# Top-32 attention and a highway layer on one core: the engines' order written out by hand, the penalty's factor moved into a matmul, two FFN products moved to VectorE

## The chip, the cores and the metric

The kernel runs on one core of a Trainium2 chip. That core has five engines with a queue each: TensorE (PE, with a row of its own for the loads of the stationary operand, PEld), VectorE (DVE), ScalarE (ACT), GpSimd (POOL) and SyncE (SP, which issues the DMA transfers here). An engine works through its queue in order. If the instruction at the head waits for another engine, everything behind it waits too. The metric is the device time of one execution in microseconds (us).

## The reference

There are 8 batches of 8 heads with 576 rows and head size 64, all float32. In each row of scores the 32 largest are kept, a softmax runs over them, and the result multiplies v. The heads, side by side, give 4608 rows of 512 numbers, the input x of the highway layer.

```python
scores = scale * np.matmul(q, k.transpose(0, 1, 3, 2))
kth = np.partition(scores, -top_k, axis=-1)[..., -top_k:-top_k + 1]
scores = np.where(scores >= kth, scores, -1000000000.0)
attn = np.exp(scores - max);  attn = attn / (sum + 1e-09)
x = (attn @ v), heads side by side
H = np.maximum(x @ w_h, 0.0)
T = 1.0 / (1.0 + np.exp(-(x @ w_t + b_t)))
out = T * H + (1.0 - T) * x
```

## The kernel before

The 576 rows of a batch are cut into four groups of 128 rows and a rest of 64. In a full group a tile is one head, in the rest group it is two heads stacked on the 128 partitions. Two tiles make a pair. A full group has 4 pairs and the rest group 2, so a batch has 18 pairs and the program 144, in 40 groups. The number `n` of a pair is its step.

These are the stages of pair `n`, with the step of the program text at which each is written:

- `scores` (step n): PE multiplies q and k into two PSUM tiles `ps` (L132), and ACT takes their positive part into `z` (L145).
- `tree` (n): DVE takes the elementwise larger of the two halves of a row, `hi`, and again of its halves, `hh` (L156, L157). POOL makes the smaller ones, `hl` and `lo`, with integer arithmetic (L161 to L164).
- `lists` (n + 1): DVE finds the 32nd largest with a chain of MAX8 and MATCH_REPLACE8 over `hh`, `hl` and `lo`, for the two tiles by turns (L176 to L197). It then multiplies it by 2^100 into `sthr` (L239).
- `settle` (n + 2, after the last pair of a group): three small POOL instructions note whether the short cut held. If it had not, an exact version would run at the end of the program. It does not run here.
- `mask` (n + 2): ACT makes a penalty `pen`, relu(2^100 * threshold - 2^100 * z), which is zero where the score is kept (L282).
- `trans` (n + 3): PE transposes `z` into PSUM (L295) and takes `pen` off with a second matmul against `nident`, minus the identity (L300), 20 matmuls in all. ACT takes exp into `et` (L312, L322).
- `av` (n + 4): PE multiplies by v, which carries a column of ones for the row sum, and ACT copies the result to `xs` (L352).
- `norm` (n + 5) and `ffn` (n + 6), after the last pair of a group: DVE takes the reciprocal of the sum and halves it (L361, L362), POOL scales to `x` (L364), PE transposes `x`, multiplies by the two weight matrices, and ACT takes relu into `h2` and tanh into `tt` (L398, L408). POOL then combines them with four instructions (L410 to L414) and SP stores the rows.
- `prep` (four times per batch): SP loads two heads of q, k and v, PE transposes q and k, ACT copies them to `kT` and `qT` and casts v.

The transposes of `prep` and all products of `ffn` share one PSUM tile, the only buffer of the pool `fps`.

The text above is not the order of the queues. A scheduler of the recording layer takes the instructions with their dependences and sorts them by a priority of its own, so on each engine stages of neighbouring steps stand mixed.

Of the kernel before, what the change touches and what calls it, by code (L numbers as in the profile page):

```python
# [23 lines left out]

class Group:
# [15 lines left out]
class Ops:  # L41


    def __init__(self, ctx, tc, shared, exact):
        self.tc, self.nc = tc, tc.nc
# [73 lines left out]
    def scores(self, n, g, pi, prep):  # L119
# [7 lines left out]
        for s0, s1 in ((0, 512), (512, S)):  # L127
            for ti, heads in enumerate(g.pairs[pi]):
                for hi, h in enumerate(heads):
# [6 lines left out]
                    )  # L136
        if self.exact:
# [8 lines left out]
        self.st[n] = dict(sc=sc)  # L146

    def tree(self, n):
# [16 lines left out]
        self.st[n]["tree"] = (hh, hl, lo)  # L165
# [52 lines left out]
    def lists(self, n, g, pi):  # L218
        nc, P, S, H = self.nc, self.P, self.S, self.H
        if pi == 0:  # L220
            for name in ("m1", "m4") if self.exact else ("m1", "m2", "m4"):
                setattr(g, name, self.lpool.tile([P, H, 8], FP32, tag=name, name=name))
            if not self.exact:
                g.sthr = self.lpool.tile([P, H], FP32, tag="sthr", name="sthr")
                g.w2 = self.lpool.tile([P, H, S // 4 + 24], FP32, tag="w2", name="w2")
# [4 lines left out]
        else:  # L230
            hh, hl, lo = self.st[n].pop("tree")
# [6 lines left out]
        if not self.exact:  # L238
# [22 lines left out]
    def mask(self, n, g, pi):  # L261
        nc, P, S = self.nc, self.P, self.S
        sc = self.st[n].pop("sc")
        z = self.zbufs[n % NZ]
        pen = None if self.exact else self.pens[n % NPEN]
        for ti in range(2):
# [14 lines left out]
            else:  # L281
# [4 lines left out]
                    bias=g.sthr[:, t : t + 1],  # L286
                    scale=-STEEP,
# [68 lines left out]
    def norm(self, g):  # L356
# [5 lines left out]
        nc.vector.tensor_scalar_mul(rinv[0:ql, :], rinv[0:ql, :], 0.5)  # L362
# [8 lines left out]
    def ffn(self, g, dst):  # L371
        nc, P = self.nc, self.P
        n_g, dm = self.n_g, self.dm
        wh, wt = self.wh, self.wt
        ql = g.qlen
        x = g.x
        xtps = self.fps.tile([P, 512], FP32, tag="fp", name="xtps")
        for i in range(n_g):
            nc.tensor.transpose(  # L379
                xtps[:, i * P : i * P + ql],  # L380
                x[0:ql, i * P : (i + 1) * P],
                self.ident[0:ql, 0:ql],
            )
        xT = self.fpool.tile([P, n_g, P], BF16, tag="xT", name="xT")
        nc.scalar.copy(
            xT[:, :, 0:ql], xtps[:].rearrange("p (g j) -> p g j", j=P)[:, :, 0:ql]
        )
        hps = self.fps.tile([P, 512], FP32, tag="fp", name="hps")
        for i in range(n_g):
            nc.tensor.matmul(  # L390
                hps[0:ql, :],
                xT[:, i, 0:ql],
                wh[:, i, :],
# [3 lines left out]
        h2 = self.fpool.tile([P, dm], FP32, tag="h2", name="h2")  # L397
        nc.scalar.activation(h2[0:ql, :], hps[0:ql, :], AF.Relu)  # L398
        tps = self.fps.tile([P, 512], FP32, tag="fp", name="tps")
        for i in range(n_g):  # L400
            nc.tensor.matmul(
                tps[0:ql, :], xT[:, i, 0:ql], wt[:, i, :], start=(i == 0), stop=False
# [4 lines left out]
        tt = self.fpool.tile([P, dm], FP32, tag="tt", name="tt")  # L407
        nc.scalar.activation(tt[0:ql, :], tps[0:ql, :], AF.Tanh)  # L408
        s1 = self.fpool.tile([P, dm], FP32, tag="s1", name="s1")
# [3 lines left out]
        o = self.fpool.tile([P, dm], FP32, tag="o", name="o")  # L413
        nc.gpsimd.tensor_add(o[0:ql, :], s1[0:ql, :], h2[0:ql, :])  # L414
        nc.sync.dma_start(dst, o[0:ql, :])
# [3 lines left out]
def kernel(  # L419
# [31 lines left out]
    nc.vector.tensor_scalar_mul(nident[:], ident[:], -1.0)  # L451
# [34 lines left out]
    with ExitStack() as cm:  # L486
        ops = Ops(cm, tc, shared, exact=False)

        def load_weights():
            for src, dst in ((moe_w_h, wh), (moe_w_t, wt)):  # L490
                for i in range(0, n_g, 2):
                    w32 = ops.fpool.tile([P, 2, dm], FP32, tag="w32", name="w32")
# [4 lines left out]
                    nc.gpsimd.tensor_copy(dst[:, i : i + 2, :], w32[:])  # L497
            bt32 = ops.fpool.tile([P, dm], FP32, tag="bt32", name="bt32")
# [3 lines left out]
            nc.sync.dma_start(bt32[:], bt_bcast)  # L502
# [41 lines left out]
        for n, (g, pi) in enumerate(pairs):  # L544
# [4 lines left out]
            if end:  # L549
                at(n + 2, ops.settle, g)  # L550
# [89 lines left out]
```

## Time and profile before

| | |
|---|---|
| three runs | median 1320.95 us (1317.99 to 1330.01) |
| the profiled execution | 1329.07 us, of which the span of the trace is 1327.3 |
| mean granted TensorE clock | 0.80 of full speed |
| busy: PE, DVE, ACT, POOL | 1031.8, 942.9, 730.7, 951.7 us |

Busy time is the time in which at least one instruction of an engine runs. Where an engine has been idle, the profile names the instruction of another engine that released it. The granted clock has two levels, 0.5 (1.2 GHz) and 1.0 (2.4 GHz), so 0.80 is a mean over stretches of both. 144 steps in 1327.3 us are 9.2 us per step.

### The profile page before, as it was taken

The page shows a single profiled execution, that of the slowest core. Times are in us where ns is not written, and L with a number is a line of the kernel's source. Part 1 is how long each engine was busy: PE and PEld are TensorE (multiplying, and loading weights), DVE is VectorE, ACT ScalarE, POOL GpSimd, SP SyncE. Part 2 cuts the span into 40 slices and gives each one's busy share as a digit, 9 for nine tenths or more (in the row PEclk, how much of TensorE's full clock was granted, in tenths as well). Part 3 has the DMA queues.
Part 4 walks back from the last instruction along what each step waited for, and adds up shares of the span by engine and source line. Part 5 has one row for each costly group of instructions (what it writes and reads, how often), then busy time and mean ns, then how long its engine had stood idle before and what let it go on. Part 6 is the DMA issues. An engine that isn't in the chain of part 4 may idle for free.

```text
span 1327.3 us, 21095 instructions
## 1 busy us (share of the span) xinstructions
PE 1031.8 (78%) x6569; PEld 599.3 (45%) x6601; DVE 942.9 (71%) x4266; ACT 730.7 (55%) x1465; POOL 951.7 (72%) x922
## 2 busy tenths in 40 slices
PE   5779796787798876878878888787876778866764
PEld 3445453444445443454444544454443444434432
DVE  6768757787677777777668776588775796676663
ACT  4566555555656555565554655565564565544442
POOL 5777867678777776777775777767677777776774
PEclk9787867878868877789786777787877888877786
DMA  4422111111101111111010111011110100000000
GB/s 103 132 56 49 26 36 31 27 26 27 44 23 27 35 26 36 22 45 27 22 31 23 41 30 31 22 23 44 27 27 13 31 15 9 9 13 9 8 9 15
DMA packets 123336, 41.56 MB, mean 31 GB/s; under 512 B 117456, under 2 KB 117456, under 8 KB 123216
## 3 DMA queue, kind: packets, MB, share of 16 engines
q1 hardware_dynamic: 123216, 40.14, 12.1%
q8 instruction: 54, 0.88, 0.3%
q14 instruction: 66, 0.54, 0.1%
HBM read 30.67 MB, written 9.44 MB: 30 GB/s over the span
## 4 chain that ended last, share of the span: by engine, by line
POOL 38%; PE 30%; DVE 19%; issue 6%; ACT 5%; SPq 1%; DMA 0%; POOLq 0%; ACTq 0%
POOL lo L163 10%; PE ps L132 10%; POOL lo L164 5%; PE zt L295 5%; POOL hl L161 5%; POOL s L410 4%; POOL hl L162 4%; DVE w L189 4%; PE hps L390 3%; DVE w L195 3%; POOL h L411 3%; PE zt L300 3%; DVE m L197 2%; DVE m L192 2%; PE xtps L379 2%
## 5 line engine op out<-in xcount | busy, mean ns | idle before, releaser
L132 PE MATMUL ps<-kT,qT 64*128 64x64 f32 (+3 forms) x1280 | 427.2, 518 | 12.3 <-ACT z L145 11.0
L282 ACT ACTIVATE pen<-z,sthr 128x576 bf16<-128x576 f32 x288 | 209.3, 770 | 276.4 <-DVE sthr L239 274.6
L295 PE MATMUL zt<-ident,z 128*128 128x128 f32 x1152 | 322.4, 336 | 0.0
L163 POOL TENSOR_TENSOR lo<-z,hi 128x576 int32<-128x576 int32 x144 | 222.0, 1546 | 115.1 <-DVE sthr L239 100.5
L300 PEld LDWEIGHTS <-pen 128*128 128x128 bf16 x1440 | 172.8, 123 | 267.5 <-ACT pen L282 235.4
L300 PE MATMUL zt<-nident,pen 128*128 128x128 bf16 x1152 | 256.6, 259 | 42.8 <-ACT pen L282 42.5
L185 DVE MAX8 w<-hl 128x8 f32<-128x72 f32 x288 | 52.4, 222 | 332.7 <-POOL hl L162 332.7
L164 POOL TENSOR_TENSOR lo<-lo,z 128x576 int32<-128x576 int32 x144 | 208.8, 1450 | 3.9
L295 PEld LDWEIGHTS zt<-ident,z 128*128 128x128 f32 x1152 | 193.4, 172 | 30.5 <-issue 5.9
L145 ACT ACTIVATE z<-ps 128x576 f32<-128x576 f32 x288 | 178.3, 650 | 51.3 <-PE ps L132 50.0
L300 PE MATMUL zr<-nident,pen 128*128 128x128 bf16 x288 | 72.1, 258 | 171.8 <-ACT pen L282 170.2
L132 PEld LDWEIGHTS ps<-kT,qT 64*128 64x128 f32 (+1 forms) x1280 | 154.1, 200 | 113.9 <-issue 63.4
L322 ACT ACTIVATE et<-zt 128x512 bf16<-128x512 f32 x288 | 170.1, 597 | 29.6 <-PE zt L300 28.1
L410 POOL TENSOR_TENSOR s<-h,x 128x512 f32<-128x512 f32 (+1 forms) x40 | 64.8, 1620 | 159.6 <-ACT h L398 159.4
L156 DVE TENSOR_TENSOR hi<-z 128x576 f32<-128x576 f32 x144 | 115.3, 803 | 19.7 <-ACT z L145 19.3
L189 DVE MAX8 w<-lo 128x8 f32<-128x288 f32 x288 | 115.4, 441 | 7.6 <-POOL lo L164 7.6
L161 POOL TENSOR_TENSOR hl<-hi,hh 128x288 int32<-128x288 int32 x144 | 116.9, 821 | 1.0 <-DVE sthr L239 1.0
L162 POOL TENSOR_TENSOR hl<-hl,hi 128x288 int32<-128x288 int32 x144 | 113.1, 794 | 0.0
L344 PEld LDWEIGHTS <-et 128*128 128x128 bf16 (+1 forms) x1600 | 79.0, 109 | 56.5 <-ACT z L145 15.4
L157 DVE TENSOR_TENSOR hh<-hi 128x288 f32<-128x288 f32 x144 | 103.1, 753 | 0.1
L312 ACT ACTIVATE et<-zr 128x256 bf16<-128x256 f32 x144 | 55.4, 385 | 79.5 <-PE zr L300 71.2
L344 PE MATMUL zr<-v,et 128*128 128x65 bf16 (+1 forms) x1600 | 97.9, 205 | 1.6 <-ACT et L322 1.1
(78 smaller groups left out, 1645.6 us busy)
## 6 DMA issues: line engine op xcount, KB each, us to landing
kin<-in_k_dram SPq DMA_DIRECT2D x64, 128.0 KB, 2.6
qin<-in_q_dram SPq DMA_DIRECT2D x64, 128.0 KB, 2.6
vin<-in_v_dram SPq DMA_DIRECT2D x64, 128.0 KB, 2.6
out_dram<-o SPq DMA_DIRECT2D x32, 256.0 KB, 2.2
kin<-in_k_dram SPq DMA_DIRECT2D x64, 16.0 KB, 2.3
qin<-in_q_dram SPq DMA_DIRECT2D x64, 16.0 KB, 2.3
vin<-in_v_dram SPq DMA_DIRECT2D x64, 16.0 KB, 2.3
w<-in_moe_w_h_dram SPq DMA_DIRECT2D x2, 512.0 KB, 4.5
```

The source lines that it names most:

```text
L132: nc.tensor.matmul(pss[ti][rows, s0:s1], qT[r, h // 2, qs : qs + g.qlen], kT[r, h // 2, s0:s1],)
L145: nc.scalar.activation(sc[:, ti, :], pss[ti][:, 0:S], AF.Relu)
L161: gp.tensor_tensor(hli, hii[:, :, 0:H2], hhi, ALU.subtract)
L162: gp.tensor_tensor(hli, hli, hii[:, :, H2:H1], ALU.add)
L163: gp.tensor_tensor(loi, sci[:, :, 0:H1], hii, ALU.subtract)
L164: gp.tensor_tensor(loi, loi, sci[:, :, H1:S], ALU.add)
L189: vec.max(w2[:, H2 + 16 : W], lo)
L282: nc.scalar.activation(pen[:, ti, 0:S], sc[:, ti, :], AF.Relu, bias=g.sthr[:, t : t + 1], scale=-STEEP,)
L295: self.nc.tensor.matmul(dst, z[:, ti, cs], self.ident[:], is_transpose=True, start=True, stop=pen is None,)
L300: self.nc.tensor.matmul(dst, pen[:, ti, cs], self.nident[:], start=False, stop=True)
L322: nc.scalar.activation(et[:, ti, 0:J, :], zt[:].rearrange("p (c j) -> p c j", c=J), AF.Exp, scale=self.scale,)
L344: nc.tensor.matmul(zr[0:ql, col : col + DE], et[:, ti, c, q0 : q0 + ql], vb[:, h, c, :], start=(c == 0), stop=(c == J),)
```

## The change

First, the order. Every PE, DVE, ACT and POOL instruction of the main path is passed to `tc.keep_in_program_order`, so the queues now stand as the text does. SP's queue is still sorted by the scheduler. The text is rewritten as one loop over steps. In step n stand: the tree and the POOL minima of pair n, the first penalty of pair n-2, `av` of n-3, the second penalty, a `prep` where one is due, scores and `z` of pair n+1, the lists of n-1, one of three FFN jobs, `trans` of n-2, `settle`, `norm`. Line 35 is the wrapper that issues all of these.

Second, the penalty. `pen` is now relu(threshold - z), and the factor 2^100 stands in `nident`. The instruction `sthr` falls away.

Third, the FFN. It is cut into jobs `ffn_x`, `ffn_h` and `ffn_t` with `ffn_o`, one job per step. DVE makes d = max(hps, 0) - x straight from PSUM, ACT writes the tanh back into PSUM, DVE makes d * (tanh + 1), and POOL makes o = (x + x) + d with two instructions. ACT's relu falls away. The halving of the reciprocal falls away too, since v's extra column now holds 2.

The weights are loaded two steps earlier, into four buffers, and cast on POOL one piece per step.

```diff
+class Pinned:
+        def issue(*args, **kw):
+            return self._tc.keep_in_program_order(fn(*args, **kw))
...
-        self.tc, self.nc = tc, tc.nc
+        self.nc = tc.nc if exact else PinnedCore(tc)
...
-            nc.vector.tensor_scalar_mul(
-                g.sthr[:, t0 : t0 + 2], g.m4[:, t0 : t0 + 2, 7], STEEP
-            )
...
-                    bias=g.sthr[:, t : t + 1],
-                    scale=-STEEP,
+                    bias=g.m4[:, t, 7:8],
+                    scale=-1.0,
...
-        nc.vector.tensor_scalar_mul(rinv[0:ql, :], rinv[0:ql, :], 0.5)
...
-        nc.scalar.activation(h2[0:ql, :], hps[0:ql, :], AF.Relu)
+        nc.vector.scalar_tensor_tensor(
+            out=g.d[0:ql, :], in0=hps[0:ql, :], scalar=0.0, in1=g.x[0:ql, :],
+            op0=ALU.max, op1=ALU.subtract,
+        )
...
-        nc.scalar.activation(tt[0:ql, :], tps[0:ql, :], AF.Tanh)
-        nc.gpsimd.tensor_add(s1[0:ql, :], h2[0:ql, :], x[0:ql, :])
-        nc.gpsimd.tensor_sub(h2[0:ql, :], h2[0:ql, :], x[0:ql, :])
-        nc.gpsimd.tensor_mul(h2[0:ql, :], h2[0:ql, :], tt[0:ql, :])
-        nc.gpsimd.tensor_add(o[0:ql, :], s1[0:ql, :], h2[0:ql, :])
+        nc.scalar.activation(tps[0:ql, :], tps[0:ql, :], AF.Tanh)
+        nc.vector.scalar_tensor_tensor(
+            out=g.d[0:ql, :], in0=tps[0:ql, :], scalar=1.0, in1=g.d[0:ql, :],
+            op0=ALU.add, op1=ALU.mult,
+        )
+        gp.tensor_tensor(o[0:ql, :], g.x[0:ql, :], g.x[0:ql, :], ALU.add)
+        gp.tensor_tensor(o[0:ql, :], o[0:ql, :], g.d[0:ql, :], ALU.add)
...
-    nc.vector.tensor_scalar_mul(nident[:], ident[:], -1.0)
+    nc.vector.tensor_scalar_mul(nident[:], ident[:], -STEEP)
...
-        nc.gpsimd.memset(vt[:], 1.0)
+        nc.gpsimd.memset(vt[:], 2.0)
...
+            if have(n):
+                ops.tree(n)
+                ops.minima(n)
+            if have(n - 2):
+                ops.mask(n - 2, *pairs[n - 2], tis=(0,))
+            if have(n - 3):
+                ops.av(n - 3, g, pi, preps[g.b][2])
+            if have(n - 2):
+                ops.mask(n - 2, *pairs[n - 2], tis=(1,))
+            if n in preparing:
+                prep(*preparing[n])
...
+            if have(n + 1):
+                ops.scores(n + 1, g, pi, preps[g.b])
+                ops.evac(n + 1)
+            if have(n - 1):
+                ops.lists(n - 1, *pairs[n - 1])
+            for job in ffn[:1]:
+                job.pop(0)()
...
+            if have(n - 2):
+                ops.trans(n - 2)
...
+                    ops.settle(g)
...
+                    ops.norm(g)
```

POOL's queue before, about one group's FFN (`s1`, `h2`, `o` are its tiles, `z4` and `z5` belong to the next two pairs):

```order
L410 TENSOR_TENSOR s1_1846<-h2_1836,x_1732 128x512
L250 TENSOR_TENSOR room_89<-m4_1477,w2_1479 128x24
L256 TENSOR_TENSOR slack_91<-m2_1476,m4_1477 128x8
L411 TENSOR_TENSOR h2_1836<-h2_1836,x_1732 128x512
L163 TENSOR_TENSOR lo_1815<-z4_73,hi_1814 128x576
L164 TENSOR_TENSOR lo_1815<-lo_1815,z4_73 128x576
L161 TENSOR_TENSOR hl_1817<-hi_1814,hh_1816 128x288
L163 TENSOR_TENSOR lo_1941<-z5_75,hi_1940 128x576
L162 TENSOR_TENSOR hl_1817<-hl_1817,hi_1814 128x288
L412 TENSOR_TENSOR h2_1836<-h2_1836,tt_1844 128x512
L161 TENSOR_TENSOR hl_1943<-hi_1940,hh_1942 128x288
L414 TENSOR_TENSOR o_1850<-s1_1846,h2_1836 128x512
```

The same engine now, two steps and the start of a third, with a group's output (`o`) and the next group's `x`:

```order
L35 TENSOR_TENSOR hl_1449<-hi_1446,hh_1448 128x288
L35 TENSOR_TENSOR hl_1449<-hl_1449,hi_1446 128x288
L35 TENSOR_TENSOR lo_1447<-z1_67,hi_1446 128x576
L35 TENSOR_TENSOR lo_1447<-lo_1447,z1_67 128x576
L35 TENSOR_TENSOR o_1515<-x_1224 128x512
L35 TENSOR_TENSOR o_1515<-o_1515,d_1414 128x512
L35 TENSOR_TENSOR hl_1549<-hi_1546,hh_1548 128x288
L35 TENSOR_TENSOR hl_1549<-hl_1549,hi_1546 128x288
L35 TENSOR_TENSOR lo_1547<-z2_69,hi_1546 128x576
L35 TENSOR_TENSOR lo_1547<-lo_1547,z2_69 128x576
L35 TENSOR_TENSOR x_1632<-xs_1237,rinv_1630 128x512
L35 TENSOR_TENSOR hl_1637<-hi_1634,hh_1636 128x288
```

Before, the minima of two pairs stand between and behind the four FFN instructions, the first of which waits for ACT's relu. Now the four minima of a pair stand together, and what depends on DVE's last work of a step (`o` with `d`, `x` with `rinv`) stands between two steps.

DVE's queue now, at the end of a step with the third FFN job (`m4` ends the chain, `hi` and `hh` begin the next step):

```order
L35 MAX m4_1479<-w3_1501 128x8
L35 MAX m4_1479<-w3_1503 128x8
L35 SCALAR_TENSOR_TENSOR d_1414<-tps_1507,d_1414 128x512
L35 TENSOR_TENSOR hi_1546<-z2_69 128x576
L35 TENSOR_TENSOR hh_1548<-hi_1546 128x288
```

Both FFN products now stand at that place, behind the chain and ahead of the tree, and wait there for PE or ACT.

PE's queue before (`ps_2967` and `ps_2968` are one pair, `ps_3086` is the first tile of the next):

```order
L295 MATMUL zt_2920<-ident_58,z0_65 128x128
L132 MATMUL ps_2967<-kT_740,qT_741 128x512
L295 MATMUL zr_2904<-ident_58,z0_65 128x128
L132 MATMUL ps_2968<-kT_740,qT_741 128x512
L132 MATMUL ps_2967<-kT_740,qT_741 128x64
L132 MATMUL ps_2968<-kT_740,qT_741 128x64
L132 MATMUL ps_3086<-kT_740,qT_741 128x512
L379 MATMUL xtps_2863<-ident_58,x_2775 128x128 x4
```

PE's queue now, in a step with a `prep` and the third FFN job:

```order
L35 MATMUL zr_2843<-v1_85,et_2842 128x65
L35 MATMUL kqps_2910<-ident_58,kin_2895 128x128 x4
L35 MATMUL kqps_2916<-ident_58,qin_2900 128x128 x4
L35 MATMUL kqps_2922<-ident_58,kin_2895 128x64
L35 MATMUL kqps_2922<-ident_58,qin_2900 128x64
L35 MATMUL ps_2929<-kT_715,qT_716 128x512
L35 MATMUL ps_2930<-kT_715,qT_716 128x512
L35 MATMUL ps_2929<-kT_715,qT_716 128x64
L35 MATMUL ps_2930<-kT_715,qT_716 128x64
L35 LDWEIGHTS xT_2749
L35 MATMUL tps_2967<-wt_96,xT_2749 128x512
```

Before, the second tile of the pair that `ps_3086` begins stood some 70 rows further on. Now the two tiles' matmuls are always neighbours, and the transposes of a `prep` stand in one block ahead of them.

## Rows read from the trace of the kernel before

**Rows 1.** The page, busy time, share of the span and instructions of each engine

```profile
PE 1031.8 (78%) x6569; PEld 599.3 (45%) x6601; DVE 942.9 (71%) x4266; ACT 730.7 (55%) x1465; POOL 951.7 (72%) x922
```

**Rows 2.** Waits: who waited for whom, us in total, times, longest us

```profile
DVE w L185 <- POOL hl L162: 332.7, 76, 10.5
ACT pen L282 <- DVE sthr L239: 274.6, 65, 8.9
...
POOL s L410 <- ACT h L398: 159.4, 37, 9.9
```

**Rows 3.** Timeline near the end: start, duration, instruction, [idle before <- releaser]

```profile
1281.73 1.82 POOL L410 TENSOR_TENSOR s<-h,x 128x512 f32<-128x512 f32 x1 [4.65 <-ACT h L398]
...
1291.98 0.37 DVE L185 MAX8 w<-hl 128x8 f32<-128x72 f32 x2 [7.61 <-POOL hl L162]
...
1297.05 0.29 PE L300 MATMUL zr<-nident,pen 128*128 128x128 bf16 x1 [9.34 <-ACT pen L282]
```

**Rows 4.** Timeline of DVE, one chain, then two trees

```profile
553.89 0.51 DVE L176 MAX8 m<-hh 128x8 f32<-128x144 f32 x2
...
556.16 0.37 DVE L185 MAX8 w<-hl 128x8 f32<-128x72 f32 x2 [0.24 <-POOL hl L162]
...
558.98 0.18 DVE L361 RECIPROCAL rinv<-xs 128x8 f32<-128x8 f32 x1
...
564.74 0.75 DVE L156 TENSOR_TENSOR hi<-z 128x576 f32<-128x576 f32 x1
565.40 0.82 DVE L157 TENSOR_TENSOR hh<-hi 128x288 f32<-128x288 f32 x2
566.14 0.51 DVE L176 MAX8 m<-hh 128x8 f32<-128x144 f32 x2
```

**Rows 5.** Timeline of DVE and POOL, trees beside POOL's two-input instructions

```profile
599.27 1.99 POOL L163 TENSOR_TENSOR lo<-z,hi 128x576 int32<-128x576 int32 x1
...
599.92 3.11 DVE L157 TENSOR_TENSOR hh<-hi 128x288 f32<-128x288 f32 x2
...
601.22 1.49 POOL L410 TENSOR_TENSOR s<-h,x 128x512 f32<-128x512 f32 x1
```

**Rows 6.** Groups by line: count, busy us, mean ns, idle us before them

```profile
L189 DVE MAX8 w<-lo 128x8 f32<-128x288 f32 x288 | 115.4, 441 | 7.6 <-POOL lo L164 7.6
...
L414 POOL TENSOR_TENSOR o<-s,h 128x512 f32<-128x512 f32 (+1 forms) x40 | 50.8, 1270 | 0.2
...
L364 POOL TENSOR_TENSOR x<-xs,rinv 128x512 f32<-128x512 f32 (+1 forms) x40 | 41.7, 1042 | 42.5 <-DVE rinv L362 38.1 <-PE ps L132 4.3
...
L239 DVE TENSOR_SCALAR sthr<-m 128x2 f32<-128x2 f32 x144 | 36.9, 256 | 0.1
```

**Rows 7.** Stretches: length, busy us (instructions) of PE, PEld, DVE, ACT, POOL, clock, DMA

```profile
50.00:1300.00 1250.00, 986.24 (x6305) 570.96 (x6337) 905.24 (x4134) 697.59 (x1397) 908.03 (x868) 0.80 0.11 28
602.70:604.27 1.57, 1.57 (x20) 1.32 (x18) 1.57 (x9) 1.33 (x3) 1.57 (x3) 1.00 0.00 0
1297.00:1299.73 2.73, 2.68 (x18) 2.00 (x18) 2.73 (x16) 1.54 (x3) 0.00 (x0) 0.50 0.00 0
```

**Rows 8.** Timeline of PE: gate matmuls, score matmuls of one tile, of two

```profile
601.61 1.04 PE L401 MATMUL tps<-wt,xT 128*128 128x512 bf16 x4
...
605.67 1.12 PE L132 MATMUL ps<-kT,qT 64*128 64x512 f32 x2
...
606.98 1.12 PE L132 MATMUL ps<-kT,qT 64*128 64x512 f32 x4
```

**Rows 9.** Timeline at the start, second `prep` of the program and what follows

```profile
14.22 1.11 PE L98 MATMUL kqps<-ident,kin 128*128 128x128 f32 x4
...
18.11 2.34 PE L132 MATMUL ps<-kT,qT 64*128 64x512 f32 x7
...
20.48 1.19 ACT L145 ACTIVATE z<-ps 128x576 f32<-128x576 f32 x2 [1.55 <-PE ps L132]
```

**Rows 10.** Timeline at the end, last MAX8 of the last chain

```profile
1300.17 0.56 DVE L197 MAX8 m<-w 128x8 f32<-128x168 f32 x2
```

More of the change, by code (lines that the diff above doesn't have):

```diff
@@ L22, with __init__, __getattr__ @@
 NPEN = 3
+class Pinned:
+    def __init__(self, tc, engine):
+        self._tc, self._engine = tc, engine
+    def __getattr__(self, name):
+        fn = getattr(self._engine, name)
+        def issue(*args, **kw):
+            return self._tc.keep_in_program_order(fn(*args, **kw))
+        return issue
+class PinnedCore:
+    def __init__(self, tc):
+        for name in ("tensor", "vector", "scalar", "gpsimd"):
+            setattr(self, name, Pinned(tc, getattr(tc.nc, name)))
+        self.sync = tc.nc.sync
 class Group:
@@ L487 @@
         ops = Ops(cm, tc, shared, exact=False)
+        weights = []
         def load_weights():
@@ L551, with have @@
-        for hp in range(1, NHP):
-            at(hp - 1, prep, 0, hp)
-        at(3, load_weights)
+        preparing = {hp - 1: (0, hp) for hp in range(1, NHP)}
         for b in range(1, B):
             for hp in range(NHP):
-                at(first[b] - 12 + 3 * hp, prep, b, hp)
-        step = 0
-        while todo:
-            for fn, args in todo.pop(step, []):
-                fn(*args)
+                preparing[first[b] - 12 + 3 * hp] = (b, hp)
+        NPR = len(pairs)
+        def have(n):
+            return 0 <= n < NPR
@@ new lines @@
+        prep(0, 0)
+        ops.scores(0, *pairs[0], preps[0])
+        ops.evac(0)
+        ffn = []
+        step = 0
+        while step < NPR + 4 or ffn:
+            n = step
+            if have(n):
[4 more added lines that the diff above has]
+            if have(n - 3):
+                g, pi = pairs[n - 3]
+                ops.av(n - 3, g, pi, preps[g.b][2])
[3 more added lines that the diff above has]
+                prep(*preparing[n])
+            if n == 1:
+                load_weights()
+            if weights and n > 2:
+                cast_weights()
+            if have(n + 1):
+                g, pi = pairs[n + 1]
+                ops.scores(n + 1, g, pi, preps[g.b])
[4 more added lines that the diff above has]
+                job.pop(0)()
+                if not job:
+                    ffn.pop(0)
+            if have(n - 2):
+                ops.trans(n - 2)
+            if have(n - 1):
+                g, pi = pairs[n - 1]
+                if pi == len(g.pairs) - 1:
+                    ops.settle(g)
+            if have(n - 3):
+                g, pi = pairs[n - 3]
+                if pi == len(g.pairs) - 1:
+                    ops.norm(g)
+                    ffn.append(
+                        [
+                            lambda g=g: ops.ffn_x(g),
+                            lambda g=g: ops.ffn_h(g),
+                            lambda g=g: (ops.ffn_t(g), ops.ffn_o(g, out_rows(g))),
+                        ]
+                    )
```

113 lines of the change are left out of this document (61 added, 52 removed).

## The prediction

> **What bounds the kernel now.** I read the busy times first [rows 1]. Over a span of 1327.3 us no engine is above 78%, and three of them stand between 71 and 78%. So no engine is full: they take turns in waiting. The list of waits says for what [rows 2]. DVE stands 332.7 us before the first MAX8 on `hl`, which POOL makes late. POOL itself stands 159.4 us at the head of its queue with the FFN's first instruction, which wants ACT's relu, while the minima that DVE needs are queued behind it. ACT then waits 274.6 us for the threshold.
>
> The timeline shows one such round from end to end [rows 3]. POOL has been idle for 4.65 us when the FFN instruction is released at 1281.73. Minima of two pairs and the rest of the FFN follow, and at 1291.98 DVE resumes after 7.61 us. At 1297.05 PE resumes after 9.34 us. The program's limit is the order in the queues, and each engine pays for it in turn.
>
> **What a step costs when nothing waits.** DVE has the most work per step after the change, so I price a step there. A chain runs from 553.89 to 558.98, with 0.24 us of idle inside: 4.85 us. A `hi` costs 565.40 - 564.74 = 0.66, a `hh` half of 566.14 - 565.40, so 0.37 [rows 4]. A step is 5.88 us, where the program now takes 9.2.
>
> **The change part by part.**
>
> *Start.* The second pair's `z` ended at 20.48 + 1.19 = 21.7 us [rows 9]. Two more steps follow that each wait for a `prep`, which takes 7.45 us from its first transpose to the end of `z` (14.22 to 21.67), and the weights' loads now stand in SP's queue ahead of the last of them. I put the beginning of step 3 at 40 us, between 21.7 + 2 x 7.45 = 36.6 and 45.
>
> *Trees and chains.* 141 trees and 142 chains remain: 141 x 1.03 + 142 x 4.85 = 834 us. `sthr` (36.9 us of DVE [rows 6]) is not in it. It was also the last link before ACT's penalty, about 0.26 us on that path in each step.
>
> *FFN on DVE.* No row shows a DVE product that reads PSUM. The nearest is `hi`, 0.66 us for 576 elements. A MAX8 of 288 takes 0.44 [rows 4, 6], and twice that is 0.88 for 576. The bounds for 512 are 0.5 and 0.8, and I take `hi`'s 0.66. With a reciprocal of 0.18, 40 x (2 x 0.66 + 0.18) = 60 us, between 47 and 71.
>
> ACT loses a relu and POOL two of four FFN instructions of 1.27 us, 40 x 2 x 1.27 = 102 us. Both have room beside DVE's step, so this buys nothing directly. It keeps POOL's load (951.7 - 102 = 850 us, 5.9 per step) just below DVE's.
>
> *Collisions of DVE and POOL.* While POOL ran a `lo` and then `s`, DVE's two `hh` took 3.11 us in place of 0.74 [rows 5, 4]. The first ended only after the `lo` had, the second after `s`. The `lo` in turn started at 599.27, when a `hi` was running, and took 1.99. So a DVE instruction with two SBUF inputs and a POOL one exclude each other, for the whole instruction, by turns. MAX8 with one input does not suffer, 441 ns in the mean although POOL is busy 72% of the time [rows 6, 1].
>
> The new order puts POOL's late work exactly where DVE's tree is. DVE's reciprocal, its second product and the last MAX8 release POOL's `x` (1.04 us), `o` (1.27) and `room` while `hi` runs, and `hh` then waits for the POOL instruction. Ahead of `o` with `d`, the instruction x + x ends about 0.5 us after DVE wants its `hi`. Per group this is 1.04 + 1.27 + 0.5 + 0.2 (my estimate for `room`) = 3.0 us, for 40 groups 120 us. The lower bound is 0, if DVE waits for `z` at that time anyway.
>
> Whether the new products collide too, no row shows. As bounds I take nothing, and 0.7 us for the one that meets x + x, 28 us in all. I take nothing, because one of their inputs is in PSUM, which makes them more like MAX8 than like `hh`. The Trainium skill (SBUF — State Buffer, section Who interferes with whom) says the same of DVE instructions with at most one SBUF input. By it the term is 0, and the sum stays as it is.
>
> *Prepared steps.* 28 steps carry a `prep` of the next batch, and all of its transposes and copies pass through the single `fps` buffer before PE reaches the step's scores. At the low clock that is 7.45 us to the end of `z` [rows 9], and ACT's two penalties stand ahead of the first copy (about 0.7 more): 8.1. At the high clock the score matmuls take 1.12 and not 2.34 [rows 8, 9] and one set of transposes half of 1.11, so 6.4. DVE wants `z` after 5.88, so 0.5 to 2.2 us are lost. In two of a batch's four such steps the gate matmuls (1.3 us from 601.61 to the end of the fifth at high clock, twice that at low) and the tanh stand between, and DVE's product, which waits for them, stands ahead of the tree: 0.7 to 1.9 more. I take 1.8 us in the mean: 50 us, between 25 and 90.
>
> *PE and its clock.* PE's 1031.8 us are 7.2 per step at a mean clock of 0.80 [rows 1, 7]. One part gets cheaper. The score matmuls of one tile alone take 1.12 us, those of two tiles side by side take 1.12 as well [rows 8]. Before they were mostly apart. I take 1.2 us off per step (one 1.12, a little more at low clock), which leaves 6.0 at 0.80. Between `trans` and `av` PE also waits about 1.0 us for the last exp. PE's own round is then 7.0 us at clock 0.80, 5.8 at 1.0 and 10.6 at 0.5. With DVE's 7.1 (5.88 plus FFN and collisions, 180 us over 144 steps) this is no longer cover but a near tie. Slack of some 2.7 us (`z` is ready that long before the tree needs it) hides single slow stretches. I add 15 us, between 0 and 145 (the third case below).
>
> *End.* From the last chain's MAX8 at 1300.17 to the end of the span are 27 us [rows 10]. The same stages follow it now, in the same dependence: 27.
>
> Sum: 40 + 834 + 60 + 120 + 50 + 15 + 27 = 1146 us of span, 1.8 more outside it: 1148 against the profiled 1329.07. The median of the runs shown is 0.6% below that execution, so I forecast **1140 us**.
>
> **The rivals.**
>
> *No collisions.* POOL's late instructions fall beside DVE's chain, or beside waits. For it: a group has one `x`, one `o` and one `room`, so some steps have none of them, and where DVE waits for `z` they cost nothing. Against it: they are released by the very instruction that stands ahead of the tree. 1146 - 120 gives a median near 1020, and less if the prepared steps cost little: 960 to 1060.
>
> *PE's clock stays as mixed as it is.* If 40% of the time goes at 0.5 and the slack doesn't cover it, steps alternate between 7.3 and 10.6 us: 1 / (0.6/7.3 + 0.4/10.6) = 8.3, or 1.0 us more on 141 steps, 1285. For it: PE's rows show 0.80 with 7.2 us of work in a 9.2 us step. Against it: PE now has pauses of about 1 us, not 9.34.
>
> *PE at 1.2 GHz nearly throughout, slower than before.* 20 matmuls of `trans` take 1.57 us in a stretch with the clock at 1.00, and 18 take 2.68 at 0.50 [rows 7]. If the pauses in every step let the clock fall and keep it down, each step takes PE's 10.6 us, and 40 + 141 x 10.6 + 27 gives about 1560. It decides where the mean step passes 9.2 us: a low share of about 0.6, a mean clock under 0.70. The Trainium skill (TensorE: Matmul & The Clock Gate, section Part 4: PE-mode transpose) says that transposes do not bring the full clock, and half of `trans` is transposes. By that rule this case would be the likely one; the stretch at 1.00 was made of `trans` alone, so the trace doesn't bear it out, though it is short.
>
> *The waits only move.* `hi` waits for `z` as long as the MAX8 waited for `hl`, because the fixed order ties all engines to the slowest of each step: 1308 to 1334. Against it: no engine has more than 7.2 us per step.
>
> That the order is not what the text says is excluded by the queues shown.
>
> **How the numbers follow.** Forecast case (1060 to 1200): 0.52. No collisions (960 to 1060): 0.23. Mixed clock (1200 to 1307): 0.17. Low clock: 0.05. Waits move: 0.03. The range of 1010 to 1280 leaves out some 0.08 below, which is part of the second case, and 0.12 above, which is the end of the third and the last two. A difference of 1% is about what can be told from none. Faster: 0.52 + 0.23 + 0.17 = 0.92, same 0.03, slower 0.05.
>
> **What would show it.** DVE's wait for `hl` should be nearly gone and DVE busy above 80% of the span. `hh` should have a mean well above 0.45 us, with the long ones in the steps with `x`, `o` and `room`. If `hh` stays near 0.45, the collisions were wrong. In prepared steps DVE should wait for `z` or for the tanh. The score matmuls should take clearly less than before, and the mean clock should be at least 0.80. The forecast is wrong upward if DVE waits for `z` in most steps and PE is the engine without idle time, and wrong downward if the mean step is below 6.6 us.

## The result, and the profile after

The changed kernel takes **1099.91 us** (median of 4 runs, 1097.74 to 1100.31), the kernel before 1324.61 us on the same chip (4 runs, 1317.99 to 1330.01). The ratio is 0.8302, 95% interval 0.8257 to 0.8348. The forecast was 1140 us, with a range of 1010 to 1280. The profiled execution has a span of 1098.5 us and a mean granted clock of 0.859.

The page, busy time, share of the span and instructions of each engine, as in [rows 1]:

```profile
PE 822.1 (75%) x6562; PEld 549.7 (50%) x6601; DVE 976.7 (89%) x4162; ACT 712.1 (65%) x1425; POOL 839.6 (76%) x842
```

One engine now stands out. DVE has hardly more work than before (976.7 against 942.9 us) but does it in 1098.5 us. It is idle for 121.8 us, where it was idle for 384.4. The page's fourth part, the chain of work that ended last by engine, says the same:

```profile
DVE 70%; PE 17%; ACT 8%; issue 3%; SPq 1%; DMA 1%; POOL 0%; ACTq 0%; DVEq 0%; POOLq 0%
```

The waits (who for whom, us in total, times, longest us), to be set beside [rows 2]:

```profile
POOL hl L35 <- DVE hh L35: 152.7, 117, 9.5
ACT pen L35 <- DVE m L35: 142.7, 81, 3.7
...
DVE hi L35 <- ACT z L35: 45.7, 12, 11.3
...
DVE d L35 <- ACT tps L35: 42.5, 17, 3.5
...
DVE d L35 <- PE hps L35: 19.0, 8, 5.0
```

DVE's 332.7 us for `hl` are gone, and so are POOL's 159.4 us for the relu. The direction has turned: POOL and ACT now wait for DVE, and that costs nothing. What DVE still waits for are `z`, the tanh (`tps`) and the relu's matmuls (`hps`), 107 us together. Of these, 28 us lie in the first four steps and 12 behind the last tree. The others lie in the steps with a `prep` alone. In the batches from the second on, DVE waits 2.94, 3.27, 1.93 and 2.53 us in a batch's four such steps (means); the first batch's four have 3.5 us together. Every other step has 0.04. Over the 28 steps with a `prep` that is 67 us.

One of these steps in the timeline (start, duration, instruction, idle before it):

```profile
478.63 1.12 PE L35 MATMUL kqps<-ident,kin 128*128 128x128 f32 x4 [2.62 <-DVE d L35]
...
480.43 1.11 PE L35 MATMUL kqps<-ident,qin 128*128 128x128 f32 x4 [0.68 <-ACT kT L35]
...
482.48 2.34 PE L35 MATMUL ps<-kT,qT 64*128 64x512 f32 x7
...
484.75 0.61 PE L35 MATMUL tps<-wt,xT 128*128 128x512 bf16 x1
...
487.16 0.58 ACT L35 ACTIVATE tps<-tps 128x512 f32<-128x512 f32 x1 [1.05 <-issue]
...
487.77 0.69 DVE L35 SCALAR_TENSOR_TENSOR d<-tps,d 128x512 f32<-128x512 f32 x1 [3.27 <-ACT tps L35]
...
488.38 0.75 DVE L35 TENSOR_TENSOR hi<-z 128x576 f32<-128x576 f32 x1
```

DVE's list ended at 484.5. On PE the `prep` stands ahead of the scores, and these ahead of the gate matmuls; the tanh follows, and the product waits for it with the tree behind it. So the wait bears the name of the tanh and was made by the `prep`.

PE itself had stood idle for 2.62 us before this `prep`, until DVE's first FFN product had been made and the `fps` buffer was free. From 477.4 to 487.6 the granted clock was 0.50. Over steps 6 to 125 its mean is 0.62 in the steps with a `prep` and 0.94 in the others.

The groups by line (busy us, mean ns, idle before), where `hi` and `hh` are the two instructions of a tree:

```profile
L35 PE MATMUL ps<-kT,qT 64*128 64x64 f32 (+3 forms) x1280 | 244.6, 509 | 0.0
...
L35 DVE TENSOR_TENSOR hi<-z 128x576 f32<-128x576 f32 x144 | 121.7, 845 | 45.7 <-ACT z L35 45.7
...
L35 DVE TENSOR_TENSOR hh<-hi 128x288 f32<-128x288 f32 x144 | 122.9, 854 | 5.0
...
L35 DVE MAX8 w<-lo 128x8 f32<-128x288 f32 x288 | 115.1, 440 | 0.0
```

In steps where POOL does nothing at that time a `hi` takes 0.745 and a `hh` 0.458 us. The rows are 121.7 + 122.9 - 144 x 1.203 = 71 us above that. MAX8 stays at 440 ns. Where most of the 71 us lie is seen in DVE and POOL's timeline over two trees:

```profile
566.87 0.71 DVE L35 TENSOR_TENSOR hi<-z 128x576 f32<-128x576 f32 x1
...
567.03 1.45 POOL L35 TENSOR_TENSOR x<-xs,rinv 64x512 f32<-64x512 f32 x1 [0.94 <-DVE rinv L35]
...
567.61 1.19 DVE L35 TENSOR_TENSOR hh<-hi 128x288 f32<-128x288 f32 x1
...
573.35 1.04 POOL L35 TENSOR_TENSOR o<-x 128x512 f32<-128x512 f32 x1
...
573.48 0.67 DVE L35 SCALAR_TENSOR_TENSOR d<-tps,d 128x512 f32<-128x512 f32 x1
...
574.07 0.93 DVE L35 TENSOR_TENSOR hi<-z 128x576 f32<-128x576 f32 x1
...
574.46 1.67 POOL L35 TENSOR_TENSOR o<-o,d 128x512 f32<-128x512 f32 x1
...
575.03 1.41 DVE L35 TENSOR_TENSOR hh<-hi 128x288 f32<-128x288 f32 x1
```

The first `hh` ends only after `x` has, the second only after `o`. In between the product `d` runs its usual 0.67 us inside POOL's x + x. The trace has one more kind that these rows don't show: some 15 of the 71 us are trees, `hi` for the most part, that meet a late `lo` of POOL's minima.

The stretch of the steady steps, to be set beside the first row of [rows 7] (length, busy us of PE, PEld, DVE, ACT, POOL, clock, DMA):

```profile
50.00:1060.00 1010.00, 775.68 (x6281) 519.93 (x6316) 938.00 (x4002) 676.87 (x1354) 798.09 (x787) 0.86 0.13 33
```

### The profile page after: what moved, and what is told of

The parts are those of the page before. It is cut to its first block, busy times and chain, and to the rows that moved or that the text cites. A ratio compares the mean times of both kernels' runs of the same rounds, so it can differ in the third digit from the quotient of the medians.

```text
span 1098.5 us, 20764 instructions
## 1 busy us (share of the span) xinstructions
PE 822.1 (75%) x6562; PEld 549.7 (50%) x6601; DVE 976.7 (89%) x4162; ACT 712.1 (65%) x1425; POOL 839.6 (76%) x842
## 4 chain that ended last, share of the span: by engine, by line
DVE 70%; PE 17%; ACT 8%; issue 3%; SPq 1%; DMA 1%; POOL 0%; ACTq 0%; DVEq 0%; POOLq 0%
DVE w L35 30%; DVE m L35 18%; DVE hh L35 9%; DVE hi L35 8%; PE ps L35 7%; PE kqps L35 5%; DVE d L35 4%; PE tps L35 2%; ACT pen L35 2%; ACT qT L35 2%; ACT kT L35 1%; PE hps L35 1%; ACT tps L35 1%; ACT z L35 1%; PE zt L35 1%
## 5 line engine op out<-in xcount | busy, mean ns | idle before, releaser
L35 ACT ACTIVATE pen<-z,m 128x576 bf16<-128x576 f32 x288 | 223.2, 775 | 142.7 <-DVE m L35 142.7
L35 PE MATMUL ps<-kT,qT 64*128 64x64 f32 (+3 forms) x1280 | 244.6, 509 | 0.0
L35 PE MATMUL zt<-ident,z 128*128 128x128 f32 x1152 | 238.1, 300 | 0.0
L35 DVE MAX8 m<-w 128x8 f32<-128x168 f32 (+1 forms) x864 | 232.6, 309 | 0.0
L35 PE MATMUL zt<-nident,pen 128*128 128x128 bf16 x1152 | 226.4, 233 | 0.0
L35 PEld LDWEIGHTS ps<-kT,qT 64*128 64x128 f32 (+1 forms) x1280 | 125.9, 206 | 104.5 <-issue 97.5
L35 DVE MATCH_REPLACE8 w<-m,w 128x144 f32<-128x144 f32 (+1 forms) x576 | 170.6, 302 | 0.0
L35 DVE TENSOR_TENSOR hi<-z 128x576 f32<-128x576 f32 x144 | 121.7, 845 | 45.7 <-ACT z L35 45.7
L35 DVE TENSOR_TENSOR hh<-hi 128x288 f32<-128x288 f32 x144 | 122.9, 854 | 5.0
L35 POOL TENSOR_TENSOR o<-o,d 128x512 f32<-128x512 f32 (+1 forms) x40 | 65.5, 1637 | 44.9 <-DVE d L35 25.4
L35 DVE MAX8 w<-hl 128x8 f32<-128x72 f32 x576 | 90.3, 217 | 0.0
```

The costliest lines, as they stand in the source:

```text
L35: return self._tc.keep_in_program_order(fn(*args, **kw))
```

## Experiments: the order or the work?

My theory was that the order makes the gain: nothing waits at the head of a queue any more with wanted work behind it. The rival was that less work makes it: no `sthr`, two POOL instructions and a relu fewer per group. I took "the order" to mean the pinned queues. The runs below were made on three chips, on which the kernel before takes 1322 to 1331 us in the median. So differences of a few us between their times mean little, and the ratio, which is taken to the kernel before on the same chip, is given beside each time.

**The order alone.** The changed kernel with the old arithmetic; the cut shows two of its parts.

```diff
-                    bias=g.m4[:, t, 7:8],
-                    scale=-1.0,
+                    bias=g.sthr[:, t : t + 1],
+                    scale=-STEEP,
...
+        gp.tensor_add(s1[0:ql, :], g.h2[0:ql, :], g.x[0:ql, :])
+        gp.tensor_sub(g.h2[0:ql, :], g.h2[0:ql, :], g.x[0:ql, :])
+        gp.tensor_mul(g.h2[0:ql, :], g.h2[0:ql, :], g.tt[0:ql, :])
+        gp.tensor_add(o[0:ql, :], s1[0:ql, :], g.h2[0:ql, :])
```

> The changed kernel's written order with the arithmetic of before: sthr on DVE, ACT's relu, all four FFN instructions of POOL, rinv halved on DVE. Theory A (the order makes the gain): against the changed kernel DVE loses 40 x 1.35 us of products (-54) and gets 144 sthr (+37) and 40 halvings (+7); POOL has two more instructions per group in its late place, where they meet the next tree (+1 to +2 us per group, +40 to +80). 1100 to 1170 us, and no large wait of DVE for hl. Theory B (less work and the shorter path make the gain): 1250 us or more.

Measured: 1138.33 us, ratio 0.8568 (0.8542 to 0.8593), and no wait of DVE for `hl`. The time is the first theory's, but the items behind it were not. DVE's rows of this kernel by line:

```profile
L35 DVE TENSOR_TENSOR hh<-hi 128x288 f32<-128x288 f32 x144 | 127.5, 886 | 4.9
...
L35 DVE TENSOR_TENSOR hi<-z 128x576 f32<-128x576 f32 x144 | 114.7, 797 | 48.1 <-ACT z L35 48.1
...
L35 DVE TENSOR_SCALAR sthr<-m 128x2 f32<-128x2 f32 x144 | 88.4, 614 | 4.9
...
L35 DVE TENSOR_SCALAR rinv<-rinv 128x8 f32<-128x8 f32 (+1 forms) x40 | 39.9, 998 | 1.3
```

`hi` and `hh` collide no more than in the changed kernel (242.2 us against 244.6). Instead two tiny instructions grew: `sthr` to 614 ns from 256 [rows 6], the halving to 998 ns. Against the changed kernel DVE gets 88.4 + 39.9 us of them, loses 54.2 of products, and is idle 82.6 us and not 121.8, because no product of DVE waits for PE or the tanh. That makes 33 us, and the spans differ by 37.

**The arithmetic alone.** The kernel before with the new arithmetic, its order left to the scheduler.

```diff
-        nc.scalar.activation(h2[0:ql, :], hps[0:ql, :], AF.Relu)
+        nc.vector.scalar_tensor_tensor(
+            out=d[0:ql, :], in0=hps[0:ql, :], scalar=0.0, in1=x[0:ql, :],
+            op0=ALU.max, op1=ALU.subtract,
+        )
...
-        nc.gpsimd.tensor_add(o[0:ql, :], s1[0:ql, :], h2[0:ql, :])
+        nc.gpsimd.tensor_tensor(o[0:ql, :], x[0:ql, :], x[0:ql, :], ALU.add)
+        nc.gpsimd.tensor_tensor(o[0:ql, :], o[0:ql, :], d[0:ql, :], ALU.add)
```

> The kernel before, its order left to the scheduler, with the new arithmetic alone: no sthr, scale in the identity, two FFN products on DVE from PSUM, two additions on POOL. Theory A: POOL's first FFN instruction no longer waits for ACT's relu but o still waits for DVE's product with minima behind it; 1240 to 1340 us, DVE's wait for hl still over 150 us. Theory B: 1100 to 1200 us.

Measured: 1310.85 us (1288.61 to 1313.51) beside 1330.64 for the kernel before. Its runs lie so far apart that no interval is given; the gain is somewhere between 1 and 3%. Its waits, in the longest of its four runs:

```profile
POOL o L411 <- DVE d L405: 178.8, 39, 10.6
DVE w L185 <- POOL hl L162: 161.2, 76, 3.7
```

POOL's FFN instruction waits as long as before, now for DVE. So the rival is out: the work that was taken away is worth 1 to 3% in the old order and, by the ratios 0.8568 and 0.8302, some 35 us in the new one, also 3%.

**The text without the pins.** The changed kernel, every queue sorted by the scheduler again.

```diff
-        self.nc = tc.nc if exact else PinnedCore(tc)
+        self.nc = tc.nc
```

> The changed kernel's text without the pinning: the scheduler sorts every engine's queue again; arithmetic and calls are the changed kernel's. If the fixed queues make the gain: POOL's o stands ahead of minima in its queue again, 1220 to 1330 us, DVE waiting over 100 us for hl. Rival (the new text, one tree and one chain per step with the FFN in three parts, suffices): 1090 to 1150 us.

Measured: **1053.28 us**, ratio 0.796 (0.7931 to 0.7989). My expectation missed by far, and what I had taken as the cause fell: without the pins the kernel is 47 us faster than with them. Its busy line and three of its waits:

```profile
PE 929.7 (88%) x6601; PEld 546.8 (52%) x6601; DVE 995.6 (95%) x4162; ACT 703.0 (67%) x1425; POOL 855.2 (81%) x842
```

```profile
DVE hi L183 <- ACT z L172: 17.5, 3, 10.6
DVE d L450 <- ACT tps L449: 17.3, 11, 3.3
DVE w L218 <- POOL hl L196: 4.9, 3, 2.1
```

DVE's wait for `hl` is 4.9 us although nothing holds POOL's queue. DVE is idle for 56.8 us, 65 less than with the pins, and its `hi` and `hh` take 267.0 us, 22 more. That is 43 of the 46 us between the spans. The new text hands the scheduler one tree and one chain per step. From the old text it makes them in twos: DVE's trees before [rows 4] and in the run with the arithmetic alone stand in pairs. Here is that run's timeline:

```profile
567.67 1.41 DVE L156 TENSOR_TENSOR hi<-z 128x576 f32<-128x576 f32 x2
...
569.00 0.82 DVE L157 TENSOR_TENSOR hh<-hi 128x288 f32<-128x288 f32 x2
```

In those kernels one tree mostly follows its neighbour after 0.7 to 1.7 us, and the next comes after some 12 to 20. In the unpinned kernel the middle half of the steps take 6.4 to 7.8 us.

**Only POOL's queue pinned.**

```diff
-        for name in ("tensor", "vector", "scalar", "gpsimd"):
-            setattr(self, name, Pinned(tc, getattr(tc.nc, name)))
+        for name in ("tensor", "vector", "scalar"):
+            setattr(self, name, getattr(tc.nc, name))
+        self.gpsimd = Pinned(tc, tc.nc.gpsimd)
```

> As the run without pinning, but with POOL's queue kept in the written order and the other three left to the scheduler. If what stood ahead of the minima on POOL made the kernel before slow: DVE's wait for hl falls under 60 us and 1120 to 1200 us. Rival (PE's, ACT's and DVE's queues count as much, the engines wait for one another in turn): within 3% of the run without any pinning, with new waits of POOL for DVE.

Measured: 1037.78 us, ratio 0.7859 (0.7823 to 0.7896), 1.5% below the run without any pin. The time is within the rival's 3%, but the question of this run had gone with the one above, for DVE hardly waited for `hl` there either. What it shows is smaller: with POOL in the written order `hi` and `hh` take 240.9 us and not 267.0, and DVE idles for 8 us more, 18 us together, and the spans differ by 17. So a pinned POOL meets DVE less often, and the pins that cost time are those of PE, ACT and DVE together; which of the three is not shown.

**The FFN in one step**, pinned otherwise as the changed kernel.

```diff
-                            lambda g=g: ops.ffn_x(g),
-                            lambda g=g: ops.ffn_h(g),
-                            lambda g=g: (ops.ffn_t(g), ops.ffn_o(g, out_rows(g))),
+                            lambda g=g: (
+                                ops.ffn_x(g), ops.ffn_h(g),
+                                ops.ffn_t(g), ops.ffn_o(g, out_rows(g)),
+                            ),
```

> The changed kernel, pinned, with a group's FFN issued whole in one step in place of in three steps. DVE's second product then stands right behind the first, with gate matmuls (1.0 to 2.1 us) and tanh (0.6) between, and PE's transposes of the step wait for DVE's first product at the step's end: 2 to 5 us per group, 1180 to 1300 us, DVE's wait for tps 80 us or more. Rival (the parting of the FFN hardly counts, the slack of the other engines takes it): 1095 to 1130 us.

Measured: 1184.75 us, ratio 0.8977 (0.8937 to 0.9016), at the low end of what was expected. DVE's wait for the tanh:

```profile
DVE d L35 <- ACT tps L35: 102.4, 40, 4.0
```

Cutting the FFN into three jobs is worth 85 us under the pins.

## Experiments: the sizes of the terms

**No additions for the output.** POOL's x + x and o + d are left out and `d` is stored, so the output lacks 2x.

```diff
-        gp.tensor_tensor(o[0:ql, :], g.x[0:ql, :], g.x[0:ql, :], ALU.add)
-        gp.tensor_tensor(o[0:ql, :], o[0:ql, :], g.d[0:ql, :], ALU.add)
-        self.nc.sync.dma_start(dst, o[0:ql, :])
+        self.nc.sync.dma_start(dst, g.d[0:ql, :])
```

> The changed kernel without POOL's two additions per group: the second product is stored, so the output lacks 2x. If DVE's tree waits for them as I read the trace (1.14 us of a group's excess in hi and hh, 40 groups): 1099 - 45 = 1055 us, between 1045 and 1068, and the excess in steps with o gone. Rival (the tree would have waited for something else in the same place, z or a chain's input): 1090 to 1100.

Measured: 1054.23 us, ratio 0.7923 (0.7898 to 0.7949): 45.7 us less, as expected. The first and the fifth step of a batch, which have an `o` and no `prep`, fall from 7.17 and 7.06 us to 6.02 and 5.91. The two tree rows fall by 38.3 to 206.3 us together, and DVE's idle time falls by 14. Of the 33 us that stay above the bare 173.2, 21 are `x` (30 of the `hh` meet it, at 0.73 us each); most of the rest are late `lo` of the minima, 10 us or so:

```profile
L35 DVE TENSOR_TENSOR hi<-z 128x576 f32<-128x576 f32 x144 | 114.6, 796 | 35.0 <-ACT z L35 35.0
...
L35 DVE TENSOR_TENSOR hh<-hi 128x288 f32<-128x288 f32 x144 | 91.7, 637 | 5.0
```

**The tanh in SBUF.** The second product gets two SBUF inputs.

```diff
-        nc.scalar.activation(tps[0:ql, :], tps[0:ql, :], AF.Tanh)
+        nc.scalar.activation(tt[0:ql, :], tps[0:ql, :], AF.Tanh)
...
-            in0=tps[0:ql, :],
+            in0=tt[0:ql, :],
             scalar=1.0,
```

> The changed kernel with the tanh written to SBUF, so that DVE's second product has two SBUF inputs; nothing else differs. If the PSUM input is why the products don't collide: the product that starts while POOL runs x + x (1.04 us) waits for it, 1.0 to 1.7 us each in place of 0.68, while hi collides less afterwards: 1105 to 1130 us. Rival (a scalar_tensor_tensor never waits for POOL, whatever its inputs): 0.6 to 0.7 us each, 1095 to 1103 us.

Measured: 1113.26 us, ratio 0.8396 (0.8372 to 0.8421). One such product in the timeline, and the row of all 40:

```profile
715.17 1.04 POOL L35 TENSOR_TENSOR o<-x 128x512 f32<-128x512 f32 x1
...
715.31 1.45 DVE L35 SCALAR_TENSOR_TENSOR d<-tt,d 128x512 f32<-128x512 f32 x1
```

```profile
L35 DVE SCALAR_TENSOR_TENSOR d<-tt,d 128x512 f32<-128x512 f32 (+1 forms) x40 | 48.0, 1200 | 37.8 <-ACT tt L35 37.7
```

27 of the 40 products meet x + x, in this kernel and in the changed one. There their median is 0.673 us with an input in PSUM, here 1.474 with both in SBUF. The other 13 take 0.684 in both. One operand's place decides it. The Trainium skill (SBUF — State Buffer, section Who interferes with whom) says so too; by that section a DVE instruction with two SBUF inputs contends with a POOL instruction that reads SBUF, and one with a single SBUF input doesn't, outside the modes in which DVE uses two ports. For this product the two runs agree on both halves.

**The last sum on DVE.** Since the second product with its PSUM input does not wait for POOL, the sum may be one more, and POOL's two additions go (not shown in the cut).

```diff
-            out=g.d[0:ql, :],
+            out=tps[0:ql, :],
             in0=tps[0:ql, :],
...
+        nc.vector.scalar_tensor_tensor(
+            out=g.o[0:ql, :], in0=g.x[0:ql, :], scalar=2.0,
+            in1=tps[0:ql, :], op0=ALU.mult, op1=ALU.add,
+        )
```

> The changed kernel with the last sum on DVE: the second product stays in PSUM (tps, in place), a third scalar_tensor_tensor makes 2x + tps into the stored tile, and POOL's two additions are gone. If a product with one input in PSUM doesn't exclude POOL: 40 x 0.68 = +27 us of DVE, -45 us of collisions (measured by the run without the additions), 1082 us, between 1072 and 1090, the product 0.66 to 0.70 us each. Rival (the third product excludes POOL as hh does, or is slower where PSUM is read and written): 1100 to 1125, the product over 0.9 us.

Measured: 1085.18 us, ratio 0.8188 (0.816 to 0.8217), 14.7 us less; the product takes 0.685 us. Time and price are as expected. That the third product doesn't exclude POOL is not shown by it, because POOL never runs beside it here.

**The `prep` behind the scores**, for all batches but the first.

```diff
-            if n in preparing:
+            if n in preparing and preparing[n][0] == 0:
                 prep(*preparing[n])
...
                 ops.evac(n + 1)
+            if n in preparing and preparing[n][0] > 0:
+                prep(*preparing[n])
```

> The changed kernel with the preparation of later batches (28 steps) issued behind the scores and their evacuation in place of ahead of them. If DVE's 75 us of idle time in these steps comes from z standing behind the preparation on PE and ACT: 1025 to 1055 us, and DVE waits in these steps under 1 us. Rival (the single fps buffer and ACT's load per step make it, the wait moves from z to tps and hps, or into the next step): 1080 to 1105.

Measured: 1072.23 us, ratio 0.806 (0.8034 to 0.8086), between the two theories. DVE's wait for `z` falls from 45.7 to 20.8 us, and the four that remain are those of the program's first steps. But those for the tanh and for `hps` stay, 54.8 us and not 61.5; 13 of the 54.8 lie behind the last tree. The 75 us of the expectation were too many, 67 is the sum over these steps, and 42 of them are left. Both theories hold in part, and that led to the next run.

**The `prep` in three parts over three steps**, each with one pass through `fps`, behind the scores as in the run above.

```diff
             nc.scalar.copy(dst_t[:, hp, 0:JP], kqps[:])
+            yield
...
-                preparing[first[b] - 12 + 3 * hp] = (b, hp)
+                for part in range(3):
+                    preparing[first[b] - 13 + 3 * hp + part] = (b, hp, part)
```

> As the run with the preparation behind the scores, but in three parts over three steps, each with one pass through the fps buffer (k, q, the rest with v); the first part one step earlier. That run left DVE 29.7 us of waits for the tanh (tps), 25.1 for the relu matmuls (hps). If three passes in one step make them: both together under 15 us and 1025 to 1050 us. Rival (any pass ahead of the FFN's matmuls makes DVE wait at its product, now in three times as many steps): 1065 to 1090.

Measured: 1040.17 us, ratio 0.7842 (0.782 to 0.7864), 59.7 us less. DVE's waits:

```profile
DVE hi L35 <- ACT z L35: 20.5, 4, 7.5
DVE d L35 <- ACT tps L35: 12.3, 10, 3.0
DVE d L35 <- PE hps L35: 7.8, 3, 3.6
```

The four waits for `z` are again those of the start. The waits for tanh and `hps` are 20.1 us. Some 12 of them lie behind the last tree, which leaves about 8 in the steps, under the 15 I had named, and the time is as expected. So three passes through the one PSUM buffer in a single step had made these waits, by the queue for the buffer or by the low clock that came with it: with the passes spread the clock rose to a mean of 0.917, and to 0.98 in the steps that had 0.62. How the 60 us are shared between the two is not shown. Pinned, with this one repair, the kernel is as fast as with POOL alone pinned.

**The weights' loads one step later.**

```diff
-            if n == 1:
+            if n == 2:
                 load_weights()
```

> The changed kernel with the five weight loads one step later, behind the loads of the last preparation of batch 0 in SP's queue. If the weights ahead of it made step 3 begin at 42.8 us: it begins at 36 to 38 us, 1093 to 1096 us. Rival (that preparation waits for its buffers of two or for PE and ACT): 42 to 43 us, 1098 to 1101 us.

Measured: 1091.71 us, ratio 0.8247 (0.8209 to 0.8285), 8 us less than the change, and step 3 begins at 36.9 us. The ratio's interval overlaps the change's own, and the profiled execution, at 1100.77 us, is the longest of its four, so it is the start in the trace that shows the effect.

**All three together**: the parted `prep`, the sum on DVE, the later loads.

> The changed kernel with the preparation in three parts behind the scores (-60 us alone), the last sum on DVE (-15) and the weights' loads one step later (-8): 1017 us, between 1008 and 1026, DVE busy 95% or more. Rival (with DVE's waits gone PE or ACT becomes the bound and the gains overlap): 1030 to 1040 us, DVE waiting for z in most steps.

Measured: **1022.66 us** (5 runs, 1021.84 to 1026.07), ratio 0.7737 (0.7712 to 0.7762), the fastest of all. The sum of the single gains, 82.6 us, was kept to 77.3.

```profile
PE 759.5 (74%) x6601; PEld 522.8 (51%) x6601; DVE 970.8 (95%) x4202; ACT 707.7 (69%) x1425; POOL 736.4 (72%) x762
```

DVE's own instructions are the limit now. In `hi` and `hh` 34 us above the bare tree remain: 21 are `x`, and most of the rest are late minima.

## Why the prediction was right, point by point

**What bounds the kernel.** That the limit was the order in the queues is right, and shown: the order alone gives a ratio of 0.8568 where the whole change gives 0.8302, the work alone gives 1 to 3%. What I did not see is that two things were changed under that name. The text in new stages, with the earlier loads of the weights that belong to it, makes the gain: the same arithmetic, sorted by the scheduler both times, takes 1288.61 to 1313.51 us from the old text and 1053.28 from the new one. The pins take 47 of it back. Which part of the text keeps the scheduler from making trees in twos stays open: it was not parted further, but for the FFN's three jobs.

**Start**: 40 us forecast, 42.79 measured, and the loads in SP's queue are the reason, as said. The timeline of DVE at the two ends:

```profile
42.79 0.76 DVE L35 TENSOR_TENSOR hi<-z 128x576 f32<-128x576 f32 x1 [7.98 <-ACT z L35]
...
1071.86 0.56 DVE L35 MAX8 m<-w 128x8 f32<-128x168 f32 x2
```

**Trees and chains**: a step with nothing else, the second of a batch, takes 5.88 us, as priced. From 42.79 to 1071.86 there are 1029 us. Without the terms below 829 are left, where 834 were forecast.

**FFN on DVE**: 60 us forecast, 27.0 + 27.2 + 7.3 (the reciprocals) = 61.5 measured, 0.67 and 0.68 us a product against 0.66. The choice that they don't collide was right, and the run with the tanh in SBUF shows why. The products by line:

```profile
L35 DVE SCALAR_TENSOR_TENSOR d<-tps,d 128x512 f32<-128x512 f32 (+1 forms) x40 | 27.2, 680 | 42.8 <-ACT tps L35 42.5
L35 DVE SCALAR_TENSOR_TENSOR d<-hps,x 128x512 f32<-128x512 f32 (+1 forms) x40 | 27.0, 674 | 19.0 <-PE hps L35 19.0
```

**Collisions**: 120 us forecast, 71 by the two rows. This is the term that was mis-sized. The place and the victim were right: `hh` has a mean of 854 ns, long in the steps with `x` and `o`. I had charged each POOL instruction in full. In a step without a `prep`, x + x and `o` cost 1.15 us (7.17 to 6.02) and not 1.77; `x` costs 0.73 in the 30 groups whose `hh` meets it, and not 1.04 in 40, since `hi` covers their first part. `room` costs nothing: 17 of the 40 run beside the first product, with its PSUM input, and where 14 others overlap the tree, `hi` and `hh` take no longer than alone. The 15 us of late minima, on the other side, were in no term of mine.

**Prepared steps**: 50 us forecast, within 25 to 90; 67 measured, 2.4 us a step against 1.8. Again the mechanism was right, with both of its branches, `z` and the tanh. In the worst step the mean is 3.27 us, where I had 0.5 to 2.2 and up to 1.9 more in two of four. One reading behind it was not what the profile says: I called the 7.45 us of [rows 9] the low clock, but for that stretch the profile gives 1.00, and the trace has no record of the clock before 31.3 us. That it was the low level I take from the seven score matmuls, 2.34 us there and 2.34 at 482.48 in the changed kernel, where the clock was 0.50.

**PE and its clock**: 15 us forecast, nothing measured outside the prepared steps. DVE idles 0.04 us in steps without a `prep`, so PE was never late there. In the prepared steps the clock was at 0.62, so a part of their 67 us belongs to it; how large a part is not shown. The line of the score matmuls fell from 427.2 us to 244.6, which is 1.27 per step against my 1.2, and the clock rose to 0.86. The line before:

```profile
L132 PE MATMUL ps<-kT,qT 64*128 64x64 f32 (+3 forms) x1280 | 427.2, 518 | 12.3 <-ACT z L145 11.0
```

**End**: 27 forecast, 1098.5 - 1071.86 = 26.6.

The errors are +3, -5, +1, -49, +17 and -15 us: 48 in all, from 1146 to 1098. Collisions and prepared steps, each off by about a third or more, cancel in part, and that is luck: the figure is better than its terms.

**What would show it.** DVE's wait for `hl` is gone and DVE is busy for 89%, `hh` is at 854 ns, the clock at 0.859, the score matmuls are cheaper, and the waits for `z` and the tanh stand in the prepared steps.

**The rivals.** No collisions: refuted by 71 us, though the time lies halfway between its range and my figure. Mixed clock and low clock: the clock was 0.859, and 0.94 in the steps without a `prep`, although half of the matmuls of `trans` are transposes. (My 1285 for the mixed clock adds its 1.0 us a step to a sum that already held 15 us for PE.) Waits only move: they moved to POOL and ACT, where they cost nothing.

## What to carry to other kernels

When no engine is full and each waits in turn, rewrite the text so that every step hands each queue one unit of work, and try it with the scheduler before fixing the queues: here the text was worth 18 to 20% and the pins cost 4%. A fixed order must also spread the rare work, such as a preparation with three passes through one PSUM buffer, over several steps. Beside a busy POOL let a two-input DVE instruction have one of its inputs in PSUM, where the measured product did not wait, and keep small TENSOR_SCALAR instructions away from POOL's, for these waited with one input (next section). Price what cannot be so by what sticks out behind its neighbour, not by its whole length.

## What the hardware showed that I had not expected

From MAX8 I had concluded that a DVE instruction with one input does not suffer from POOL. `sthr` and the halving have one input of 2 and 8 elements, and they do. In the run with the order alone, DVE and POOL in the timeline:

```profile
644.07 1.41 POOL L35 TENSOR_TENSOR lo<-z,hi 128x576 int32<-128x576 int32 x1
...
644.79 0.71 DVE L35 TENSOR_SCALAR sthr<-m 128x2 f32<-128x2 f32 x1
...
645.42 0.19 DVE L35 RECIPROCAL rinv<-xs 128x8 f32<-128x8 f32 x1
...
645.56 1.41 POOL L35 TENSOR_TENSOR lo<-lo,z 128x576 int32<-128x576 int32 x1
...
645.64 1.35 DVE L35 TENSOR_SCALAR rinv<-rinv 128x8 f32<-128x8 f32 x1
```

Each ends with the POOL instruction beside it. `sthr` takes 0.17 us where no POOL instruction is under way as it starts (45 times) and 0.90 in the median where one is (99 times); the halving takes 0.16 us alone and 1.35 in the median beside POOL. RECIPROCAL (0.19 us beside `lo`) and MAX8 (440 ns in the mean) with as many inputs don't wait. The Trainium skill (SBUF — State Buffer, section Who interferes with whom) names tensor_scalar among the operations that can take the ports shared with POOL, and these waits fit that. So in the new order the two tiny instructions took 128 us of DVE, where the old rows had 37 for `sthr`.
